# Places of their own for the sums and copies of the first channel product, and long rows for its weight sums in DRAM

## The chip, the cores and the metric

The kernel runs on one core of a Trainium2 chip. The metric is the device time of one execution in microseconds (us), as a median of several runs; less is better. The engines of a core are called here by the names that the profile uses: PE (TensorE, the matmuls; PEld are its weight loads), DVE (VectorE), ACT (ScalarE), POOL (GpSimd) and SP (SyncE, which here only issues DMAs). DMAs are issued by SP, by ACT and by POOL[...].

## What is computed

An attention block whose mask comes from hashes of the queries and keys, and after it an MLP mixer with a token part and a channel part. The change lies in the channel part, the last two lines:

```python
xt = x.transpose(0, 2, 1)                       # x: attention output, 4 x 768 rows of 512
h = np.maximum(xt @ w_tok1, 0.0) @ w_tok2       # token part
u = x + h.transpose(0, 2, 1)
h2 = np.maximum(u @ w_ch1, 0.0) @ w_ch2         # channel part: 512 -> 1536 -> 512
return (u + h2).astype(np.float32)
```

All data are float32. In the kernel u lies transposed in SBUF as the tile XT, 128 partitions by 4 blocks of channels by 3072 rows.

## The kernel before

Attention takes about the first 320 us, the token part follows until about 404 us, and the channel part, the function `channels`, runs from 404 us to the end. It works in three groups of 1024 rows (s = 0, 1, 2). Each group has two products: the first channel product (512 to 1536, then a ReLU, into the four tiles R) and the second (1536 to 512, in `outputs`).

**Fewer multiplications by sums.** Both products are split 2 x 2 in the manner of Strassen and Winograd: seven products of half-size blocks in place of eight, p1 to p7, with sums and differences of the weights on the one side, of the data on the other, and of the results. In groups 1 and 2 the first product is split a second time for four of its seven (p2, p6, p3, p4, the list `SMALLER`), and in all groups the second product is for six of its seven. The sums of weights for this second level are made once, in group 0, by DVE (`prepare`), and written to DRAM: `left_...` for the second product (`passed`), `hidden_left_...` for the first (`hidden_passed`). Later groups fetch them from there.

**Group 0** runs `hidden(0, t)` for six blocks t. A block has seven accumulations in PSUM; ACT copies three of the results (p1, p5, p7) and the sum u into SBUF (`copy`, L714 and L716), DVE adds them into R (L746, L755), POOL adds p5 and p7 (L750). In between, at two places for each t, DVE runs one of eleven jobs of `prepare`. A job of `parts` makes four sums (L986 to L989) in a place and hands it to a store. There are two such places: the tile `seen`, and, where `other` is true, a piece of `area(1)`. SP then issues the DMAs to DRAM: for the second weights L997 and L999, for the first L1006 (three DMAs for the sums, one for each t) and L1011 (four for the blocks that need no sum).

**Groups 1 and 2** run `hidden_pair(s, t)` for three t, each over two blocks at once. A pair computes p1 whole, then the four smaller products with a class `Smaller`, whose steps are `one`, `three`, `rest` and `finish`. `one` starts a bank of PSUM and lets ACT copy its first part into a place e (L827); `rest` lets PE add into the same bank, and then fetches the weight sums of the product that comes five later (`fetch_hidden_left`, L788), into one of five slots in WC1 and SW1. The copies of a pair are p1, p5 and u (L880), e2 and e6 (L827), and e3 and e4, which take the places of p1 and e2 again.

**Where they lie.** Two large SBUF tiles, area(0) and area(1), stand at the places that the second weights and their sums had (WC2 and SW2). Each holds, in its first 2688 columns, the weight sums of one of the six split products (`left_at`, filled by L1047 two products ahead, 1344 KB each), and behind them blocks of results: `output_at(0)`, `(1)` and `(2)` in area(0), `output_at(3)` in area(1), and behind that a scratch piece `extra`. In `outputs` these blocks are q7, q57 (later q4), q6 (later q3) and q5 (later q2). q57, q3, q2 and q4 are added to the output in DRAM by POOL's DMAs (L1151 in `store`), the last of them, q4, after the last product of a group, by L1186 and L1187:

```python
add(q4, q4, q7)()
store(q4, 1, 0)()
```

The next group's first pair then takes its places by

```python
p1, e2, u, e6, p5 = [output_at(i).rearrange("p i n -> p (i n)") for i in (0, 2, 3, 1)] + [flat_q1]
```

so that p1 is where q7 was, e2 where q3 was, u where q2 was, e6 where q4 was, and p5 where q1 was.

**What sets the order.** The program is written out in order by hand (`manual_schedule`): every engine takes its instructions in the order of the text, and an instruction waits until what it reads is written and what it overwrites has been read, by whatever engine or DMA. In pools, tiles of one tag share a number of places (`bufs`), and a new tile waits for the last use of the one that had its place. PSUM is cut into four pairs of banks that go round (`ring`). SP's queue holds nearly all fetches and stores in the order of the text. POOL's queue holds the stores of L1151 and the fetches of `look` (L1226): 384 KB of the queries or keys, which ACT squares and sums later (L1215, L1216), to find out whether the fast attention was safe. Were it not, a second, careful version of everything would run (the `If` at the end); with these inputs it does not.

Of the kernel before, what the change touches and what calls it, by code (L numbers as in the profile page):

```python
# [48 lines left out]
def kernel(  # L49
# [13 lines left out]
    nc = tc.nc  # L63
# [617 lines left out]
    def channels(pool, psum, SW1, second, TA, judge):  # L681
# [6 lines left out]
        q1 = pool.tile([P, KC, TT], F32, name="q1", tag="q1", bufs=1)  # L688
        last = B * S // (2 * TT) - 1

        def copies(name):
            return pool.tile([P, TT], F32, name=name, tag="c", bufs=6)


        ring = [0, 1, 2, 3]
# [15 lines left out]
                    skip_group_check=True,  # L711
                )

        def copy(ps, name, shape=None):  # L714
            c = copies(name)
            nc.scalar.copy(c if shape is None else shape(c), ps)  # L716
            return c if shape is None else shape(c)

        def split(a):
            return a.rearrange("p (n t) -> p n t", n=2)  # L720
# [8 lines left out]
        def hidden(s, t):  # L729


            sl = [slice(TT * (2 * s + i), TT * (2 * s + i) + TT) for i in range(2)]
            low, high = slice(P * t, P * t + P), slice(DCH // 2 + P * t, DCH // 2 + P * t + P)
            ks = range(KC)
            r = [a[:, :, t] for a in R]
            ps = [b[:, i] for b in blocks(2) for i in range(2)]
            accumulate(ps[0], lambda k: WC1[:, k, low], lambda k: XT[:, k, sl[0]], ks)
            accumulate(ps[1], lambda k: WC1[:, KC + k, low], lambda k: XT[:, KC + k, sl[0]], ks)
            accumulate(ps[2], lambda k: WC1[:, k, high], lambda k: T[0][:, k], ks)
            accumulate(ps[3], lambda k: SW1[:, 1, k, low], lambda k: T[2][:, k], ks)  # L740
            p1 = copy(ps[0], "p1")
            p5 = copy(ps[2], "p5")
            accumulate(ps[0], lambda k: SW1[:, 0, k, low], lambda k: T[1][:, k], ks, False)
            p7 = copy(ps[3], "p7")
            end_rows()
            nc.vector.tensor_tensor(r[0], split(ps[1]), split(p1), op=ALU.add)  # L746
            nc.vector.tensor_scalar(r[0], r[0], 0.0, None, op0=ALU.max)
            for job in jobs.pop(0) if jobs else []:
                job()
            nc.gpsimd.tensor_tensor(p7, p5, p7, op=ALU.add)  # L750
            accumulate(ps[2], lambda k: SW1[:, 2, k, low], lambda k: XT[:, KC + k, sl[1]], ks, False)
            accumulate(ps[3], lambda k: WC1[:, KC + k, high], lambda k: T[3][:, k], ks, False)
            u = copy(ps[0], "u")
            for k, a in [(3, p7), (1, ps[2]), (2, ps[3])]:
                nc.vector.tensor_tensor(r[k], split(a), split(u), op=ALU.add)  # L755
            nc.vector.tensor_scalar(r[1], r[1], 0.0, None, op0=ALU.max)

            def end():
                for k in (3, 2):
                    nc.scalar.activation(r[k], r[k], ACT.Relu)  # L760

            unfinished.append(end)
            nc.vector.tensor_tensor(r[1], r[1], r[0], op=ALU.subtract)
# [21 lines left out]
        def fetch_hidden_left(h):  # L785

            if h < 4 * GP * last:
                nc.sync.dma_start(out=hidden_left_at(h), in_=hidden_passed[SMALLER[h % 4]][:, h // 4 % GP, : 7 * P])  # L788

        def hidden_left_at(h):  # L790

# [14 lines left out]

        def kept(name):

            a = hidden_passed[name]
            return [a[:, :, P * i : P * i + P] for i in range(4, 8)]  # L810

        def rows_of(a):

            return a[:, 0].rearrange("p (t c) -> p t c", t=GP)

        class Smaller:

# [37 lines left out]
        def hidden_pair(s, t, between):  # L855


            sl = [slice(TT * (2 * s + i), TT * (2 * s + i) + TT) for i in range(2)]
            ks = range(KC)
            r = [a[:, :, t::GP].rearrange("p n i c -> p i n c") for a in R]  # L860
            x, z, e, y = ring
            ring[:] = [y, e, x, z]
            p1, e2, u, e6, p5 = [output_at(i).rearrange("p i n -> p (i n)") for i in (0, 2, 3, 1)] + [flat_q1]
            e3, e4 = p1, e2
            h = 4 * GP * (s - 1) + 4 * t
            p2, p6, p3, p4 = [Smaller(h + i, name, s) for i, name in enumerate(SMALLER)]

            def rows(a):
                return a.rearrange("p (i n c) -> p i n c", i=2, n=2)

            def banks(a):
                return a.rearrange("p i (n c) -> p i n c", n=2)

            def whole(pair, left, right, which=(0, 1)):
                for i in which:
                    at = P * (t + GP * i)
                    accumulate(pair[:, i], lambda k: left(k)[:, at : at + P], right, ks)

            def copy(to, pair):
                nc.scalar.copy(to.rearrange("p (i n) -> p i n", i=2), pair)  # L880

            def plus(to, a, b):
                nc.vector.tensor_tensor(to, a, b, op=ALU.add)

            def relu(i):
                nc.scalar.activation(r[i], r[i], ACT.Relu)

            X = bank_pair(x)
            whole(X, lambda k: WC1[:, k], lambda k: XT[:, k, sl[0]])
            Z, E = bank_pair(z), bank_pair(e)  # L890
            copy(p1, X)
            p2.one(E, e2)
            p2.three(Z, True)
            Y = bank_pair(y)
            whole(Y, lambda k: WC1[:, k, DCH // 2 :], lambda k: T[0][:, k], [0])
            n = TT * 3 // 2
            plus(p1[:, :n], Z.rearrange("p i n -> p (i n)")[:, :n], p1[:, :n])
            end_rows()
            p2.rest()
            whole(Y, lambda k: WC1[:, k, DCH // 2 :], lambda k: T[0][:, k], [1])  # L900
            p2.finish()
            copy(p5, Y)
            look()
            plus(r[0], rows(p1), rows(e2))
            for job in between:
                job()
            E = bank_pair(z)
            p6.one(E, e6)
            p6.three(X)
            copy(u, X)  # L910
            V = bank_pair(e)
            whole(V, lambda k: SW1[:, 1, k], lambda k: T[2][:, k])
            p6.rest()
            look()
            plus(rows(p5), banks(V), rows(p5))
            p6.finish()
            relu(0)
            plus(u, u, e6)
            E3 = bank_pair(x)
            p3.one(E3, e3)  # L920
            look()
            p3.three(Y)
            p4.three(V)
            p4.one(bank_pair(z), e4)
            plus(r[1], banks(Y), rows(u))
            plus(r[2], banks(V), rows(u))
            plus(r[3], rows(p5), rows(u))
            p3.rest()
            p4.rest()
            p3.finish()  # L930
            plus(r[1], r[1], rows(e3))
            p4.finish()
            plus(r[2], r[2], rows(e4))
            look()

            def end():
                relu(3)
                relu(1)
                relu(2)
                nc.vector.tensor_tensor(r[1], r[1], r[0], op=ALU.subtract)  # L940

            unfinished.append(end)
# [3 lines left out]
        SMALLER = ["p2", "p6", "p3", "p4"]  # L946
        GP = HC // 2
        hidden_passed = second["hidden_passed"]
        flat_q1 = q1.rearrange("p i n -> p (i n)")

# [7 lines left out]
        def prepare():  # L960
# [33 lines left out]
            def second_parts(name):  # L994
# [3 lines left out]
                    for i, a in enumerate(raw):  # L998
                        nc.sync.dma_start(out=to[:, 4 + i].rearrange("p (k c) -> p k c", k=QC), in_=a)  # L999

                return parts(left[name], store)

            def hidden_parts(name):
                def store(place, raw, rest):
                    for t in range(GP):
                        nc.sync.dma_start(  # L1006
                            out=hidden_passed[name][:, t, : 4 * P].rearrange("p (i c) -> p i c", i=4),
                            in_=place[:, :, P * t : P * t + P],
                        )
                    for there, here in zip(kept(name), [*raw, rest]):  # L1010
                        nc.sync.dma_start(out=there, in_=rows_of(here))  # L1011

                return parts(first_weight(name), store, SMALLER.index(name) % 2 == 0)

# [70 lines left out]
        def product(s, j, name, q, between, final=None):  # L1085
# [13 lines left out]

            part(0, 4, b00)  # L1100
            part(1, 5, b10)
            p1 = copy(ps[0], "p1", lambda c: c[:, half])
            nc.vector.tensor_tensor(b00, b11, b01, op=ALU.subtract)  # L1103
            part(2, 0, b01)
            part(3, 1, extra())
            nc.vector.tensor_tensor(b10, b10, b00, op=ALU.subtract)
            p57 = copy(pairs[1][:, :, half], "p57", lambda c: c.rearrange("p (i t) -> p i t", i=2))
            part(0, 2, b00, False)
            part(2, 3, b11, False)
            u = copy(ps[0], "u", lambda c: c[:, half])  # L1110
            if s < last:
                look()
            part(3, 6, b10, False)
# [133 lines left out]
        if not judge:  # L1247
            for name in SMALLER:
                (a00, a01), (a10, a11) = weight_quarters(first_weight(name))
                for there, here in zip(kept(name), [a00, a01, a11, a10]):  # L1250
                    nc.sync.dma_start(out=rows_of(here), in_=there)
        for t in range(HC):
            if t == 1:
                residual(0)
# [23 lines left out]
    def with_token_weights(stage):  # L1278
        with tc.tile_pool(name="tok", bufs=1, reuse_waits="tile") as tok:
# [7 lines left out]
    n = NHT // 4 * P  # L1287
    second = {
        "hidden_passed": {
            f"p{i}": dram.tile([P, NHT // 4, 8 * P], F32, name=f"hidden_left{i}") for i in (2, 3, 4, 6)  # L1290
        },
        "passed": {
            f"p{i}": dram.tile([P, (4 if i == 1 else 7) * n], F32, name=f"left{i}") for i in range(1, 8)
# [95 lines left out]
```

## Time and profile before

The median of three runs is 825.07 us (824.71 to 825.82). The profiled execution has a span of 823.8 us.

| engine | busy, us | share of the span | instructions |
|---|---|---|---|
| PE | 807.6 | 98% | 3901 |
| DVE | 665.2 | 81% | 869 |
| ACT | 423.4 | 51% | 675 |
| POOL | 42.6 | 5% | 69 |

| DMA issues of the part concerned | number | KB each |
|---|---|---|
| `second<-left` (L1047) | 18 | 1344 |
| `left<-seen` (L997) | 6 | 768 |
| `left<-second` (L999) | 18 | 192 |
| `hidden_left<-second`, `hidden_left<-seen` (L1006) | 6 + 6 | 256 |
| `hidden_left<-WC`, `hidden_left<-SW` (L1011) | 8 + 8 | 192 |
| `WC<-hidden_left`, `SW<-hidden_left` (L788) | 15 + 9 | 448 |
| `out<-second` from POOL (L1151) | 11 | 512 |

How to read it. In the names of the profile, `out<-in` is what an instruction writes and reads; buffer numbers are left out, so that `second` stands for area(0), area(1), WC2 and SW2 alike, `b` for the PSUM banks, `p` and `u` for the copies of `hidden` and `product`, and `q` for q1. A bracket at the end of a line of the timeline, such as [0.56 <-DVE R L1103], says how long the engine stood idle before this line, and what ended the wait. A part of a line that reads "x14" is a run of 14 instructions merged. A float32 matmul shows as two instructions. "To landing" is the time from the issue of a DMA to its completion.

### The profile page before, as it was taken

The page shows a single profiled execution, that of the slowest core. Times are in us where ns is not written, and L with a number is a line of the kernel's source. Part 1 is how long each engine was busy: PE and PEld are TensorE (multiplying, and loading weights), DVE is VectorE, ACT ScalarE, POOL GpSimd, SP SyncE. Part 2 cuts the span into 40 slices and gives each one's busy share as a digit, 9 for nine tenths or more (in the row PEclk, how much of TensorE's full clock was granted, in tenths as well). Part 3 has the DMA queues.
Part 4 walks back from the last instruction along what each step waited for, and adds up shares of the span by engine and source line. Part 5 has one row for each costly group of instructions (what it writes and reads, how often), then busy time and mean ns, then how long its engine had stood idle before and what let it go on. Part 6 is the DMA issues. An engine that isn't in the chain of part 4 may idle for free.

```text
span 823.8 us, 10610 instructions
## 1 busy us (share of the span) xinstructions
PE 807.6 (98%) x3901; PEld 473.6 (57%) x3901; DVE 665.2 (81%) x869; ACT 423.4 (51%) x675; POOL 42.6 (5%) x69
## 2 busy tenths in 40 slices
PE   9999999999999999999999999997999998999996
PEld 4444444444444444455544458865666885675885
DVE  4889898999988676798486869985769896777985
ACT  5777788888887774121022321335773333775111
POOL 1000000000000000000011110111100011100001
PEclk9999999999999999999999999999999999999999
DMA  4445454546524235561028895696644577630455
GB/s 159 140 142 169 136 156 138 162 156 207 146 89 118 80 79 189 173 212 39 0 76 293 245 329 191 197 311 179 239 143 141 222 202 179 224 121 1 148 182 112
DMA packets 79915, 132.31 MB, mean 161 GB/s; under 512 B 29608, under 2 KB 51568, under 8 KB 77552
## 3 DMA queue, kind: packets, MB, share of 16 engines
q1 hardware_dynamic: 73744, 112.60, 41.4%
q0 software_dynamic: 5552, 18.35, 9.1%
q8 instruction: 33, 0.54, 0.3%
q10 hardware_dynamic: 560, 0.61, 0.2%
q14 instruction: 26, 0.21, 0.1%
HBM read 97.21 MB, written 33.69 MB: 159 GB/s over the span
## 4 chain that ended last, share of the span: by engine, by line
PE 76%; issue 16%; DMA 2%; DVE 2%; POOL 2%; ACT 1%; POOLq 0%; ACTq 0%; DVEq 0%
PE b L709 28%; PE sc L345 19%; PE acc L392 16%; PE t L623 5%; PE t L642 5%; PE sums L416 2%; DMA out<-second 1%; PE hp L306 1%; DMA second<-left 1%; POOL seen L1226 1%; POOL out L1151 1%; DVE second L1145 1%; PE hw L324 0%; PE idle L454 0%; POOL looked L1226 0%
## 5 line engine op out<-in xcount | busy, mean ns | idle before, releaser
L352 ACT ACTIVATE e<-sc 128x768 f32<-128x768 f32 x192 | 153.1, 812 | 13.2 <-PE sc L345 12.3
L345 PE MATMUL sc<-qk 64*128 64x384 f32 x768 | 158.5, 492 | 0.3 <-ACT e L352 0.3
L709 PE MATMUL b<-R,second 128*128 128x256 f32 (+1 forms) x612 | 151.2, 404 | 1.1 <-DVE R L1103 0.6
L709 PEld LDWEIGHTS b<-R,second 128*128 128x128 f32 x612 | 116.1, 190 | 33.3 <-issue 18.6
L392 PE MATMUL acc<-e,vn 128*64 128x384 f32 x768 | 130.9, 490 | 0.0
L384 DVE TENSOR_TENSOR esd<-esd,e 128x768 f32<-128x768 f32 x128 | 122.3, 955 | 10.4 <-ACT e L352 0.5
L716 ACT COPY p<-b 128x512 f32<-128x512 f32 (+1 forms) x54 | 27.2, 516 | 158.3 <-PE b L709 158.3
L345 PEld LDWEIGHTS sc<-qk 64*128 64x128 f32 x768 | 66.5, 187 | 55.6 <-issue 45.2
L392 PEld LDWEIGHTS acc<-e,vn 128*64 128x64 f32 x768 | 52.3, 137 | 74.9 <-issue 74.3
L709 PE MATMUL b<-XT,WC 128*128 128x256 f32 (+1 forms) x264 | 84.2, 464 | 4.6 <-ACT second L827 4.6
L709 PEld LDWEIGHTS b<-XT,WC 128*128 128x128 f32 x264 | 51.2, 194 | 35.0 <-issue 24.6
L345 PE MATMUL sc<-bits 64*128 64x384 bf16 x384 | 62.9, 323 | 0.2 <-DVE bits L328 0.2
L623 PE MATMUL t<-x,W 128*128 128x512 f32 x96 | 41.8, 593 | 0.0
L642 PE MATMUL t<-W,r 128*128 128x384 f32 x128 | 41.8, 486 | 0.0
L398 ACT ACTIVATE num<-acc,vsum 128x384 f32<-128x384 f32 x32 | 18.6, 582 | 41.6 <-PE acc L392 41.2
L437 ACT COPY rec<-rec 32x384 f32<-32x384 f32 x64 | 32.6, 509 | 12.9 <-DVE rec L431 12.4
L709 PE MATMUL b<-XT,SW 128*128 128x256 f32 (+1 forms) x120 | 36.4, 440 | 2.1 <-ACT second L827 2.1
L380 DVE SCALAR_TENSOR_TENSOR esd<-e 128x768 f32<-128x768 f32 x32 | 30.5, 954 | 9.3 <-ACT e L352 9.3
L642 PEld LDWEIGHTS t<-W,r 128*128 128x128 f32 x128 | 24.3, 190 | 17.6 <-issue 1.4
L345 PEld LDWEIGHTS <-bits 64*128 64x128 bf16 x384 | 19.3, 94 | 25.4 <-DVE bits L328 0.8
L709 PE MATMUL b<-TA,WC 128*128 128x512 f32 x72 | 33.8, 592 | 0.0
L709 PE MATMUL b<-TA,SW 128*128 128x512 f32 x72 | 32.9, 592 | 0.0
(170 smaller groups left out, 1064.6 us busy)
## 6 DMA issues: line engine op xcount, KB each, us to landing
second<-left SPq DMA_DIRECT2D x18, 1344.0 KB
raw<-in_moe_w_ch SPq DMA_DIRECT2D x16, 768.0 KB
qk<-in_qk SPq DMA_DIRECT2D x15, 768.0 KB
seen<-in_qk POOLq DMA_DIRECT2D x21, 384.0 KB, 4.0
WC<-hidden_left SPq DMA_DIRECT2D x15, 448.0 KB
vn<-in_v SPq DMA_DIRECT2D x16, 384.0 KB
vt<-in_vT SPq DMA_DIRECT2D x16, 384.0 KB
bounced<-stage SPq DMA_DIRECT2D x32, 192.0 KB
```

The source lines that it names most:

```text
L345: nc.tensor.matmul(sc[:, i, :HALF], t[rows, 1, P * c : P * c + P], t[rows, 0, qs], start=start, stop=not start,)
L352: nc.scalar.activation(e, sc[:, :, :HALF], ACT.Exp, scale=SCALE)
L380: nc.vector.scalar_tensor_tensor(self.d, es[0], NR * EPS, es[1], op0=ALU.add, op1=ALU.add,)
L384: nc.vector.tensor_tensor(self.d, self.d, e, op=ALU.add)
L392: nc.tensor.matmul(acc[D * i : D * i + D], vn[:, i, c], e[:, i], start=(c == 0), stop=(c == NR - 1),)
L398: nc.scalar.activation(nums[self.n][:, self.half], acc, ACT.Identity, scale=-1.0, bias=vsum,)
L416: nc.tensor.matmul(ps[at : at + 32], ones[:, :32], self.halves[h].d[:, i], start=True, stop=True,)
L437: nc.scalar.copy(rec[other : other + 32, h], rec[at : at + 32, h])
L623: nc.tensor.matmul(ps, W1[:, r, P * j : P * j + P], x[:, r], start=(r == 0), stop=(r == NR - 1),)
L642: nc.tensor.matmul(ps[:, :HALF], r1[:, j, P * cb : P * cb + P], W2[:, j, HALF * half : HALF * half + HALF], start=(j == 0), stop=(j == NJ ...
L709: nc.tensor.matmul(ps, left(k), right(k), start=start and k == ks[0], stop=stop and k == ks[-1], skip_group_check=True,)
L716: nc.scalar.copy(c if shape is None else shape(c), ps)
```

## The change

It does four things.

1. The tag `c`, of which the copies are tiles, has 3 places of 1024 columns and no longer 6 of 512. A hidden block of group 0 takes two tiles and cuts each in half, for p1, p5 and p7, u. A product of `outputs` takes one and cuts it into p1 (a quarter), p57 (a half) and u (a quarter); before, it took three tiles.
2. In a hidden pair, p5, e6 and u are three such tiles. Only p1 and e2 (and e3 and e4 after them) stay in `output_at`.
3. The sums of p2 of the second weights are made in the piece of area(1) and not in `seen`, so that `seen` and the piece alternate from there on.
4. The DRAM tiles of the first product's weight sums are laid out as 8 rows of 384 columns in each partition, and no longer as 3 blocks of 8 x 128. A store of the sums is then one DMA with whole rows, a store of a block without sums has rows of 384 columns (1.5 KB), not of 128 (512 bytes); a fetch reads seven pieces of 128 columns for each partition, where it read 896 columns in one piece.

It is for the waits at the places that are stored from, and for the number of pieces that the stores to DRAM are cut into.

```diff
-        def copies(name):
-            return pool.tile([P, TT], F32, name=name, tag="c", bufs=6)
+        def copies():
+            return pool.tile([P, 2 * TT], F32, name="c", tag="c", bufs=3)
...
-        def copy(ps, name, shape=None):
-            c = copies(name)
-            nc.scalar.copy(c if shape is None else shape(c), ps)
-            return c if shape is None else shape(c)
+        def copy(ps, c):
+            nc.scalar.copy(c, ps)
+            return c
...
-            p1 = copy(ps[0], "p1")
-            p5 = copy(ps[2], "p5")
+            c = [a[:, TT * i : TT * i + TT] for a in (copies(), copies()) for i in range(2)]
+            p1 = copy(ps[0], c[0])
+            p5 = copy(ps[2], c[1])
...
-            p7 = copy(ps[3], "p7")
+            p7 = copy(ps[3], c[2])
...
-            u = copy(ps[0], "u")
+            u = copy(ps[0], c[3])
...
-                nc.sync.dma_start(out=hidden_left_at(h), in_=hidden_passed[SMALLER[h % 4]][:, h // 4 % GP, : 7 * P])
+                t = h // 4 % GP
+                nc.sync.dma_start(
+                    out=hidden_left_at(h).rearrange("p (i c) -> p i c", i=7),
+                    in_=hidden_passed[SMALLER[h % 4]][:, :7, P * t : P * t + P],
+                )
...
-            a = hidden_passed[name]
-            return [a[:, :, P * i : P * i + P] for i in range(4, 8)]
+            return [hidden_passed[name][:, i] for i in range(4, 8)]
...
-            p1, e2, u, e6, p5 = [output_at(i).rearrange("p i n -> p (i n)") for i in (0, 2, 3, 1)] + [flat_q1]
+
+            p1, e2 = [output_at(i).rearrange("p i n -> p (i n)") for i in (0, 2)]
+            p5, e6, u = copies(), copies(), copies()
...
-                return parts(left[name], store)
+                return parts(left[name], store, name == "p2")
...
-                    for t in range(GP):
-                        nc.sync.dma_start(
-                            out=hidden_passed[name][:, t, : 4 * P].rearrange("p (i c) -> p i c", i=4),
-                            in_=place[:, :, P * t : P * t + P],
-                        )
+                    nc.sync.dma_start(out=hidden_passed[name][:, :4], in_=place)
                     for there, here in zip(kept(name), [*raw, rest]):
-                        nc.sync.dma_start(out=there, in_=rows_of(here))
+                        nc.sync.dma_start(out=there, in_=here[:, 0])
...
-            p1 = copy(ps[0], "p1", lambda c: c[:, half])
+            c = copies()
+            p1 = copy(ps[0], c[:, half])
...
-            p57 = copy(pairs[1][:, :, half], "p57", lambda c: c.rearrange("p (i t) -> p i t", i=2))
+            p57 = copy(pairs[1][:, :, half], c[:, TT // 2 : TT * 3 // 2].rearrange("p (i t) -> p i t", i=2))
...
-            u = copy(ps[0], "u", lambda c: c[:, half])
+            u = copy(ps[0], c[:, TT * 3 // 2 :])
...
-            f"p{i}": dram.tile([P, NHT // 4, 8 * P], F32, name=f"hidden_left{i}") for i in (2, 3, 4, 6)
+            f"p{i}": dram.tile([P, 8, NHT // 4 * P], F32, name=f"hidden_left{i}") for i in (2, 3, 4, 6)
```

More of the change, by code (lines that the diff above doesn't have):

```diff
@@ L807, in kept @@
         def kept(name):
-            a = hidden_passed[name]
-            return [a[:, :, P * i : P * i + P] for i in range(4, 8)]
-        def rows_of(a):
-            return a[:, 0].rearrange("p (t c) -> p t c", t=GP)
+            return [hidden_passed[name][:, i] for i in range(4, 8)]
         class Smaller:
@@ L948, in channels @@
         hidden_passed = second["hidden_passed"]
-        flat_q1 = q1.rearrange("p i n -> p (i n)")
         ORDER = ["p1", "p5", "p7", "p6", "p3", "p2", "p4"]
@@ L1250, in channels @@
                 for there, here in zip(kept(name), [a00, a01, a11, a10]):
-                    nc.sync.dma_start(out=rows_of(here), in_=there)
+                    nc.sync.dma_start(out=here[:, 0], in_=there)
         for t in range(HC):
```

## The prediction

> **What bounds the kernel now.** I read the engines' busy time first, then the stretches in which TensorE is not full, then who ended each gap.
>
> The profile page, part 1 and one line of part 5 (idle before it and releaser at the right):
>
> ```profile
> PE 807.6 (98%) x3901; PEld 473.6 (57%) x3901; DVE 665.2 (81%) x869; ACT 423.4 (51%) x675; POOL 42.6 (5%) x69
> ...
> L709 PE MATMUL b<-XT,WC 128*128 128x256 f32 (+1 forms) x264 | 84.2, 464 | 4.6 <-ACT second L827 4.6
> ```
>
> TensorE (PE) is the bound, so the change is worth what PE stands idle, plus what a slow clock costs after a gap. The busy time by stretch (start:end, length, then PE, weight load, VectorE, ScalarE, GpSimd, granted clock, DMA share, GB/s):
>
> ```profile
> 470.00:480.00 10.00, 10.00 (x24) 4.37 (x23) 3.95 (x8) 2.71 (x5) 2.37 (x2) 1.00 1.04 303
> 480.00:500.00 20.00, 18.90 (x72) 13.20 (x71) 18.77 (x27) 3.69 (x7) 1.10 (x2) 1.00 1.06 340
> ...
> 540.00:560.00 20.00, 17.66 (x59) 10.69 (x57) 14.76 (x25) 6.59 (x11) 3.60 (x4) 1.00 0.91 262
> 560.00:580.00 20.00, 17.75 (x62) 12.96 (x63) 12.51 (x14) 13.91 (x23) 1.66 (x3) 0.91 0.70 234
> ...
> 680.00:700.00 20.00, 17.89 (x56) 10.77 (x56) 13.00 (x24) 7.30 (x13) 3.57 (x4) 0.96 0.75 184
> ```
>
> From 380 us to 800 us PE is otherwise full in every row. It lacks 1.10 us at 480 to 500, 2.34 + 2.25 = 4.59 us around 560, and 2.11 us before 700; the clock falls just after the last two. The timeline names the releasers (start, length, engine, what):
>
> ```profile
> 492.38 4.12 PE L709 MATMUL b<-R,second 128*128 128x256 f32 x18 [0.56 <-DVE R L1103]
> 497.05 4.12 PE L709 MATMUL b<-R,second 128*128 128x256 f32 x18 [0.55 <-DMA second<-left]
> ...
> 555.61 1.21 POOL L1151 DMA_DIRECT2D out<-second  x1 [7.34 <-DVE XT L775]
> 561.82 0.37 ACT L827 COPY second<-b 128x256 f32<-128x256 f32 x1 [6.47 <-DMA out<-second]
> 562.25 4.83 PE L709 MATMUL b<-XT,WC 128*128 128x256 f32 x14 [4.59 <-ACT second L827]
> ...
> 691.58 1.21 POOL L1151 DMA_DIRECT2D out<-second  x1 [8.82 <-DVE second L853]
> 697.59 0.37 ACT L827 COPY second<-b 128x256 f32<-128x256 f32 x1 [4.00 <-DMA out<-second]
> 698.02 4.98 PE L709 MATMUL b<-XT,SW 128*128 128x256 f32 x14 [2.12 <-ACT second L827]
> ```
>
> Read upwards, the big gaps are one chain, once at each of the two group boundaries. GpSimd issues the adding store of block q4 (L1151 for L1187) at 555.61; it lands at about 561.75, since the chain of waits has a piece of 6.13 us for it (5.93 us at the second). ScalarE's copy for e6 (L827, from p6.one) goes to `output_at(1)`, the place that q4 is stored from, so it waits. PE's p6.rest adds into the bank that this copy reads, so PE waits too.
>
> [...] a gap of 2.12 us also costs clock here, so I count both. [...] at 470 to 480, mostly 512-byte stores, 303 GB/s at a share of 1.04. No line here shows a 512-byte read from DRAM.
>
> **Part 1: e6, u and p5 in tiles of their own (L863).** e6 leaves q4's place, u leaves q2's (`output_at(3)`), p5 leaves q1. Same copies, same sizes: no work added. When would e6's copy start? ScalarE's work before it, the second half of a look, starts at 555.17 and takes 0.19, so it is free at 555.36; the copy takes 0.37 and ends about 555.8. PE ends its eight 512-wide matmuls (554.07, 3.60 long) at 557.66. So e6 is ready 1.9 us early and the gap closes: 4.6 us, and 2.1 us at the second boundary. The clock: 14 matmuls of 256 columns took 4.83 and 4.98 us; 12 in full clock take 2.75 (at 613.41), so 14 take 3.2. That is 1.6 + 1.8 = 3.4 us more.
>
> What waits next? I walked the pair on. The u copy ends at 556.8 and a look at 558.8, when p6.rest is through (559.0); the three copies of p6, p3 and p4 then end before PE asks, as in the pairs for t = 1, 2, where PE has no gap. e2 stays in `output_at(2)`, from which q3 is stored: issued 535.15, median landing 7.5 us, 542.7; e2 is copied at 547.03, 4.3 us to spare. The three new tiles were last read by the product before (L1137, done 544.78); p5's copy is at 552.54. No wait.
>
> **Part 2: copies as halves and quarters of 3 tiles of 1024 instead of 6 of 512.** Same bytes and instructions. A product now uses one tile of three, not three of six. A hidden block uses two of three, so a tile returns after 1.5 blocks, as before. ScalarE's u waited for L746 (16.4 us in 5 waits), the reader of p1: apparently it took p1's slot. It now shares a tile with p7 instead. PE was full all through 400 to 480, so: nothing.
>
> **Part 3: sums of p2 (second weights) to area(1).** VectorE's sums wait for the previous store of the one place "seen": five waits, 11.3 us in all. Two alternating places shorten this. The new wait is for the old tile of area(1), SW2: its last store is issued by 444.92 and p2's sums ran at 450.92, so 6 us to spare (a similar store released VectorE 3.3 us after issue). Behind these sums on VectorE stand the adds of the hidden block (L746, L755), and PE waits for those only a block (12 us) later. Worth nothing by itself.
>
> **Part 4: long rows for the hidden sums' stores.** Per name: before, 3 + 4 issues with 12 x 128 + 4 x 384 = 3072 rows of 512 B; after, 1 + 4 issues with 128 rows of 6 KB and 512 of 1.5 KB. SyncE (SP) time falls from 4.46 us (1.81 + 2.65 at 484.46) to about 5 x 0.33 = 1.7, by the 0.33 us of a 128-row issue. This touches the first gap. VectorE sat 6.43 us at 480.96 for a hidden store, and L1103 ended 0.56 us late. SP issued the last hidden store until 488.96, and only then (489.07) the fetch of p7's weights, which took 7.85 us and came 0.55 late; p1's matmuls, which free its place, end about 486.6. With VectorE 6 us and the fetch 2.4 us earlier both waits close: 1.1 us. No clock loss there.
>
> **Part 5: the price, reads in 512-byte pieces (L788).** 24 fetches of 448 KB (459 KB decimal) go from 128 rows of 3.5 KB to 896 of 512 B. Lower bound: 459 KB at 414 GB/s (545 to 550, full DMA) = 1.1 us. Upper bound: one row costs the same however short, 7 times that, 7.8 us; the stores speak against it (303 GB/s). I take the stores' rate: 1.5 us, and keep 3.0 as a doubtful end. PE uses up one fetch in 5.6 us (two pairs, 8 fetches, from 571.23 to 616.00 = 44.8 us); four others lie ahead in the ring; DMA share at 580 to 620 is 0.60 and 0.48. Even 3.0 us a fetch fits. The first five are issued from 532.65 behind a fetch of 768 KB (786 KB decimal); at 229 GB/s (532 to 536) the first lands at about 538.5, and is used at about 546. SP needs about 1 us for each, from the 0.57 us of a 512-row store: hidden, its next issue is at 542.64. What hides the cost: PE's own work.
>
> **Sum.** 1.1 + 4.6 + 2.1 + 3.4 = 11.2 us. I keep 0.3 for short waits of the kind of PEld on L850 (0.7 us in three). 825.07 - 10.9 = **814.2 us**.
>
> **Rivals.**
> (a) All gaps close: 814.2. Chance 0.76.
> (b) Another wait takes over in part: the pairs begin earlier, but a look's data may not. The look fetched at 556.37, behind q4's store, would be wanted at 565.5, not 571.70; at its median landing of 6.4 us it comes at 562.8, at the longest of 7.9 still in time. ScalarE runs its queue in order, so a late one holds the copies behind it. If each boundary keeps 1.5 us, 814.2 + 3 = 817.2, or 818.9 with one clock loss. For it: DMA is full (1.03) at 545 to 550. Chance 0.14.
> (c) Nothing gained: the copies still wait for the store through the way that the three tiles are handed out, and part 4 alone counts: 824. Against: the tiles' readers are done 8 us before. Chance 0.03.
> (d) Short reads are the new bound, slower: at three times the stores' cost, 4.5 us a fetch, nine fetches in 540 to 580 add some 9 x 3.1 = 28 us of DMA time where only 40 x 0.195 = 8 us are free; if three quarters of that 20 us reach PE, 814.2 + 15 = 829. Chance 0.07.
>
> **Numbers.** Faster 0.76 + 0.14 + 0.01 of (c) = 0.91; same 0.02; slower 0.07. The range runs from 813.0 (nothing kept back, a run's spread) to 819.0, the end of (b).
>
> **What would show it.** Right: no wait of ScalarE's L827 on `out<-second`, PE full at 540 to 580 and 680 to 700 with clock 1.00, the p7 fetch issued near 486.6, no VectorE wait on hidden_left, DMA share in the pairs up by no more than a tenth. Wrong: PE waiting for `WC<-hidden_left` or `SW<-hidden_left`, or ScalarE waiting for `seen` and `looked` at their squares (L1215), or e2's copy waiting for q3's store.

## The result, and the profile after

The changed kernel takes **813.68 us** (813.58 to 814.83), the kernel before 824.97 us beside it: a ratio of 0.9865, with a 95% interval of 0.9847 to 0.9882. That is 11.3 us less; 814.2 us was forecast. The experiments below ran on other chips, on which the kernel before took some 826.5 us with a wider spread. So they are read by their ratio to it and, where single microseconds matter, by the gaps in their profiles.

The profile page of the changed kernel, part 1 and the line of part 5 that showed the wait:

```profile
PE 803.6 (99%) x3901; PEld 471.6 (58%) x3901; DVE 664.1 (82%) x869; ACT 423.1 (52%) x675; POOL 42.5 (5%) x69
...
L709 PE MATMUL b<-XT,WC 128*128 128x256 f32 (+1 forms) x264 | 82.5, 456 | 0.0
```

The span fell from 823.8 to 811.9, by 11.9 us. PE's idle time, the span less its busy time, went from 16.2 to 8.3: 7.9 us, against 7.8 us of gaps forecast to close. Its busy time for the same 3901 matmuls fell by 4.0. Of this, 3.5 us lie in the two lines of part 5 that hold the 14 matmuls after the big gaps (XT,WC from 84.2 to 82.5, XT,SW from 36.4 to 34.6): the clock that the gaps had cost, with a granted clock of 0.91 at 560 to 580 and 0.96 at 680 to 700 before and of 1.00 in both now. The other 0.5 us is within the spread of kernels that have none of the gaps, whose PE busy times run from 802.6 to 804.0.

The stretches, in the columns of the prediction (PE's busy time is the second number):

```profile
470.00:480.00 10.00, 10.00 (x25) 4.49 (x24) 6.66 (x12) 3.97 (x7) 1.96 (x2) 1.00 0.99 388
480.00:500.00 20.00, 20.00 (x78) 14.60 (x77) 15.81 (x21) 2.71 (x5) 1.10 (x2) 1.00 0.68 238
...
540.00:560.00 20.00, 20.00 (x71) 13.10 (x70) 15.29 (x27) 10.60 (x19) 4.17 (x5) 1.00 0.92 242
560.00:580.00 20.00, 20.00 (x70) 13.10 (x69) 14.14 (x16) 14.21 (x24) 1.94 (x4) 1.00 0.99 314
...
680.00:700.00 20.00, 20.00 (x74) 13.87 (x73) 16.26 (x24) 13.36 (x23) 3.46 (x5) 1.00 0.89 213
```

PE is full at a clock of 1.00 in each. At 470 to 480 the DMA engines move 388 GB/s at about the share that gave 303 before. How much of that is the long rows isn't shown: the long rows alone, tried below, gave 317 there.

At the first boundary the timeline reads (lines of ACT, PE and POOL, in order of time):

```profile
545.63 0.38 ACT L826 COPY second<-b 128x256 f32<-128x256 f32 x1
...
553.87 0.35 ACT L826 COPY c<-b 128x256 f32<-128x256 f32 x1
...
556.11 3.19 PE L709 MATMUL b<-XT,WC 128*128 128x256 f32 x14
...
556.64 1.21 POOL L1148 DMA_DIRECT2D out<-second  x1 [11.53 <-issue]
...
564.98 0.84 ACT L1212 ACTIVATE looked<-looked 128x768 f32<-128x768 f32 x1 [0.96 <-DMA looked<-in_qk]
```

e6 (L826, now into c) is copied at 553.87, before q4's store is even issued (556.64), and PE goes on at 556.11 without a bracket. Its 14 matmuls take 3.19 us where they took 4.83. The first line is e2, still in q3's old place, the last a look that came 0.96 us late; both come up again.

The chain of waits from 440 to 805 us is now PE alone:

```profile
439.62 329.04 PE b L709 x1226
768.66 0.11 PE b L1235
768.77 36.28 PE b L709 x168
```

### The profile page after: what moved, and what is told of

The parts are those of the page before. It is cut to its first block, busy times and chain, and to the rows that moved or that the text cites. A ratio compares the mean times of both kernels' runs of the same rounds, so it can differ in the third digit from the quotient of the medians.

```text
span 811.9 us, 10567 instructions
## 1 busy us (share of the span) xinstructions
PE 803.6 (99%) x3901; PEld 471.6 (58%) x3901; DVE 664.1 (82%) x869; ACT 423.1 (52%) x675; POOL 42.5 (5%) x69
## 3 DMA queue, kind: packets, MB, share of 16 engines
q1 hardware_dynamic: 82320, 112.60, 42.4%
## 4 chain that ended last, share of the span: by engine, by line
PE 99%; DVE 0%; ACT 0%; issue 0%; ACTq 0%
PE b L709 49%; PE sc L345 20%; PE acc L392 16%; PE t L623 5%; PE t L642 5%; PE sums L416 2%; PE hp L306 1%; PE hw L324 1%; PE idle L454 0%; ACT vt L297 0%; ACT e L352 0%; ACT g L311 0%; DVE second L1128 0%; DVE g L310 0%; DVE bits L326 0%
## 5 line engine op out<-in xcount | busy, mean ns | idle before, releaser
L715 ACT COPY c<-b 128x512 f32<-128x512 f32 (+1 forms) x78 | 37.4, 488 | 187.7 <-PE b L709 174.2
L709 PE MATMUL b<-XT,WC 128*128 128x256 f32 (+1 forms) x264 | 82.5, 456 | 0.0
L437 ACT COPY rec<-rec 32x384 f32<-32x384 f32 x64 | 32.6, 509 | 12.9 <-DVE rec L431 12.4
L709 PE MATMUL b<-XT,SW 128*128 128x256 f32 (+1 forms) x120 | 34.6, 422 | 0.0
```

Of the source, the lines that this page charges most:

```text
L437: nc.scalar.copy(rec[other : other + 32, h], rec[at : at + 32, h])
L709: nc.tensor.matmul(ps, left(k), right(k), start=start and k == ks[0], stop=stop and k == ks[-1], skip_group_check=True,)
L715: nc.scalar.copy(c, ps)
```

## The experiments

The theory is that of the prediction: e6's place held PE at both boundaries, and the stores of the hidden weight sums held the fetch of p7's weights. The first rival is that less work for the DMA engines let q4's store land in time; the second, that u or p5 was the holder; the third, that the short reads cost something.

**The places alone, and the rows alone.** The first kernel is the changed one without its parts 3 and 4, the second the kernel before with these two alone.

```diff
# places alone, against the changed kernel
-                    out=hidden_left_at(h).rearrange("p (i c) -> p i c", i=7),
-                    in_=hidden_passed[SMALLER[h % 4]][:, :7, P * t : P * t + P],
+                nc.sync.dma_start(out=hidden_left_at(h), in_=hidden_passed[SMALLER[h % 4]][:, h // 4 % GP, : 7 * P])
...
-                return parts(left[name], store, name == "p2")
+                return parts(left[name], store)
```

> The new places and the tiles of 1024 alone (parts 1 and 2); rows in DRAM and the place of p2's sums as before. Theory: the two large gaps and the clock loss after them go, the first gap (1.1 us at 480 to 500) stays: 825.0 - 10.1 = about 814.9, with the p7 fetch still issued near 489. Rival (the DMA relief of the long rows is what lets the store of q4 land in time): about 824, with ScalarE still waiting for the store.

> Long rows and p2's place alone (parts 3 and 4); the sums and copies of the pairs stay in the stored blocks. Theory: only the first gap closes, and the store of q4 lands a little later because the fetches now read 512-byte pieces: between 824 and 827, and perhaps slower than before. Rival (DMA relief closes the gaps): near 814.

Measured: the places alone, ratio 0.9872 (0.9836 to 0.9908); the rows alone, 0.9984 (0.9973 to 0.9996). PE's timeline, first with the places alone, then with the rows alone:

```profile
497.44 2.83 PE L709 MATMUL b<-R,second 128*128 128x256 f32 x12 [1.26 <-DMA second<-left]
```

```profile
562.91 5.50 PE L709 MATMUL b<-XT,WC 128*128 128x256 f32 x14 [6.79 <-ACT second L826]
...
698.83 3.29 PE L709 MATMUL b<-XT,SW 128*128 128x256 f32 x14 [1.59 <-ACT second L826]
```

With the places alone the first gap stays, and it is the only one. With the rows alone it goes, and the two others stay. They shift, from 4.59 and 2.12 to 6.79 and 1.59 us. At the first boundary PE asks 1.5 us earlier (556.12 for 557.66), and q4's store is issued 1.1 us later (556.75 for 555.61), because q2's store before it took 12.4 us to land, 8.2 in the kernel before. So relief of the DMA engines did not bring q4's store in time; the first rival falls. The first gap is too small to be seen in the times: the places alone lie within the interval of a repeat of the whole change on the same chip, below (0.9855, 0.9813 to 0.9898).

**Which place.** The changed kernel with e6 back, with u back, and with u and p5 back:

```diff
-            p1, e2 = [output_at(i).rearrange("p i n -> p (i n)") for i in (0, 2)]
-            p5, e6, u = copies(), copies(), copies()
# e6 back
+            p1, e2, e6 = [output_at(i).rearrange("p i n -> p (i n)") for i in (0, 2, 1)]
+            p5, u = copies(), copies()
# u back
+            p1, e2, u = [output_at(i).rearrange("p i n -> p (i n)") for i in (0, 2, 3)]
+            p5, e6 = copies(), copies()
# u and p5 back
+            p1, e2, u = [output_at(i).rearrange("p i n -> p (i n)") for i in (0, 2, 3)]
+            p5 = q1.rearrange("p i n -> p (i n)")
+            e6 = copies()
```

> The changed kernel with e6 alone back in q4's place. Theory: e6 is the one copy that holds. In the changed kernel q4's store lands at 563.5 (556.6 + 6.9) and at 689.7 (683.7 + 6.0), the matmuls before it end at 556.1 and 688.0: gaps of about 7.7 and 2.2 us, and 1.7 us of clock after each, so about 827, slower than before the change. Rival (u's or p5's place was the holder): 813.7, no gap.

> The changed kernel with u alone back in q2's place. The store of q2 lands at 556.3 (543.9 + 12.4), u is copied at 554.1 in the changed kernel: ScalarE is held 2.2 us at the first boundary; at the second q2's store lands at 683.4, before u at 686.0: no wait. Theory: up to 1.5 us of PE gap, 813.7 to 816. Rival (u's place is worth as much as e6's): 820 or more.

> The changed kernel with p5 back in q1 and u back in q2's place: of the pairs' copies only e6 has a place of its own. Theory: the whole gain of the two large gaps is e6's, so this is the changed kernel's time (813.7 to 815 on the first chip), with ScalarE held about 1.4 us for u at the first boundary and PE full. Rival (p5 or both places count): 816 or more.

Measured: e6 back, ratio 0.9976 (0.996 to 0.9992); u back, 0.9849 (0.9815 to 0.9883); u and p5 back, 0.9847 (0.9823 to 0.9871). PE with e6 back:

```profile
562.63 6.00 PE L709 MATMUL b<-XT,WC 128*128 128x256 f32 x14 [6.66 <-ACT second L826]
...
699.29 3.29 PE L709 MATMUL b<-XT,SW 128*128 128x256 f32 x14 [1.84 <-ACT second L826]
```

ACT with u and p5 back, the copy of u:

```profile
555.31 1.01 ACT L882 COPY second<-b 128x1024 f32<-128x1024 f32 x1 [1.52 <-DMA out<-second]
```

e6's place alone makes or breaks the gain of the two large gaps. u does wait for q2's store when it lies there, 1.5 us, and PE does not notice; its span is 811.9 us, that of the changed kernel. The size was missed for e6 back: 827 was expected, which is a span of some 825.2 (the time less 1.8 us); the profile has 823.1. The store landed at 562.1 and not 563.5, and the second gap, 1.84 us, cost no clock (1.00 at 680 to 720). The sum of the spans does close: 811.9 + 6.66 + 1.84 + 2.8 (14 matmuls in 6.00 instead of 3.19) = 823.2.

**What closes the first gap.** The kernel before with the long rows alone (part 4 of the change, as its diff shows it), with p2's place alone (part 3), and the changed kernel without the long rows (parts 1 to 3):

```diff
# p2's place alone, against the kernel before
-                return parts(left[name], store)
+                return parts(left[name], store, name == "p2")
```

> Only the rows in DRAM changed (part 4), p2's sums and all copies where they were. Theory: the first gap is the long stores' doing, so it closes (no wait of VectorE above 2 us for hidden stores, the p7 fetch issued near 486.7, PE full at 480 to 500); the later gaps as with both (6.8 and 1.6 us): 823 in the profile. Rival (the place of p2's sums closes it): about 1.1 us of gap at 480 to 500 stays.

> Only p2's sums moved to the piece of area(1) (part 3). Theory: VectorE waits less for the stores of the second weights (11.3 us before, about 8.7 with it), but the short rows still hold the last hidden job and the issue of the p7 fetch: the gap at 480 to 500 stays at 0.5 to 1.3 us, 824 in the profile. Rival: the gap closes.

> The changed kernel with the old layout in DRAM (parts 1 to 3, short rows stored, 3.5 KB read in one piece). Moving p2's sums alone closed the first gap, and so did the long rows alone. Theory: either is enough, so the time of the changed kernel, PE full at 480 to 500. Rival (with PE earlier the short stores hold the p7 fetch again): a gap of 0.5 to 1.3 us at 497.

Measured: long rows 0.9987 (0.9967 to 1.0008), inconclusive as a time; p2's place 0.9968 (0.9952 to 0.9985); parts 1 to 3, 0.9848 (0.9827 to 0.9869), as good as the whole change. The row 480 to 500 of each:

```profile
480.00:500.00 20.00, 20.00 (x72) 13.49 (x71) 18.81 (x27) 3.61 (x6) 1.10 (x2) 1.00 0.87 330
```

```profile
480.00:500.00 20.00, 20.00 (x76) 14.14 (x75) 18.74 (x26) 3.88 (x7) 1.10 (x2) 1.00 0.96 310
```

```profile
480.00:500.00 20.00, 19.96 (x80) 14.80 (x79) 17.36 (x23) 2.72 (x5) 1.10 (x2) 1.00 0.86 289
```

The third expectation held, the second failed: p2's place alone closes the gap too. The first held in the main, but VectorE still waits 3.6 us for the hidden stores there (6.4 before), not under 2. With p2's place alone it waits 2.3.

The same work stands up to 4 us apart in these traces, so times are counted from the first matmul of the second product. With p2's place, and then with the long rows alone, this matmul and SP's issue of p7's fetch read:

```profile
477.56 14.35 PE L709 MATMUL b<-R,second 128*128 128x512 f32 x42
...
488.06 0.48 SPq L1047 DMA_DIRECT2D second<-left  x1
```

```profile
479.18 14.35 PE L709 MATMUL b<-R,second 128*128 128x512 f32 x42
...
489.68 0.32 SPq L1042 DMA_DIRECT2D second<-left  x1
```

The fetch is issued 10.5 us after that matmul in both, as in every run without the gap (10.5 in the changed kernel, with the rows alone and with parts 1 to 3). It is 12.9 us in the kernel before (489.07 - 476.18) and 13.0 with the places alone. So each part brings the fetch forward by the whole 2.4 us, to where the matmuls of p1 leave its place free, and no part can bring it further. With p2's place SP is done with the hidden stores only 0.2 us before (487.86), with the long rows 2.5 us (487.20). The parts are not additive: each closes the same 1.1 us, and the second one adds nothing.

**The price of short reads.** First, each fetch cut into 14 pieces in each partition:

```diff
-                    out=hidden_left_at(h).rearrange("p (i c) -> p i c", i=7),
-                    in_=hidden_passed[SMALLER[h % 4]][:, :7, P * t : P * t + P],
+                    out=hidden_left_at(h).rearrange("p (i c) -> p i c", i=14),
+                    in_=hidden_passed[SMALLER[h % 4]][:, :7, P * t : P * t + P].rearrange(
+                        "p i (j c) -> p i j c", j=2
+                    ),
```

> The changed kernel with every fetch of the first product's weight sums cut into 256-byte pieces, 14 for each partition in place of 7. In the trace the 256-byte packets of other transfers took 18.6 ns and the 512-byte ones 29, so a fetch should cost 112 x 18.6 = 2.1 us of all engines in place of 56 x 29 = 1.6. Theory: still hidden, 813.7 to 815; the stores of q2 and q4 and the looks land a little later. Rival (short reads are close to being the bound): 818 or more, with PE waiting for the weights or ScalarE for the looks.

The trace has the same 21,504 packets of 512 bytes as the changed kernel, and the DMA share at 540 to 580 is 0.96 in both: neighbouring halves were joined again, so this is a repeat (0.9855, 0.9813 to 0.9898) and says nothing of the price. The changed kernel itself was run again with the third group above:

> The changed kernel as it is, on the same chip as the two others, to compare them by: 813.7 if this chip is like the first; the two others within 1 us of it.

It gave 0.985 (0.9828 to 0.9871), and u and p5 back, and parts 1 to 3, lie within 0.4 us of its median. The short reads were then tried with pieces that do not lie side by side. These reads bring as many bytes, but from other columns, so the kernel goes without the right weight sums, and only its time counts:

```diff
-                    out=hidden_left_at(h).rearrange("p (i c) -> p i c", i=7),
-                    in_=hidden_passed[SMALLER[h % 4]][:, :7, P * t : P * t + P],
+                    out=hidden_left_at(h).rearrange("p (i c) -> p i c", i=28),
+                    in_=hidden_passed[SMALLER[h % 4]][:, :7].rearrange("p i (j t c) -> p (i j) t c", j=4, t=GP)[:, :, t],
```

> The changed kernel with each fetch of the first product's weight sums read as 28 pieces of 128 bytes for each partition, three pieces apart in DRAM, so that they can't be joined (the pieces of 256 bytes in the earlier run lay side by side and were joined). The bytes are as many, but they belong to other columns, so the weights of groups 1 and 2 are not the right ones; only the time is of interest. 448 KB are then 3584 pieces, 224 for each of 16 engines. The trace shows 18.6 ns for a 256-byte packet and 29 for one of 512; a line through the two gives 13.4 ns for 128 bytes, so 3.0 us a fetch in place of 1.6, the doubtful end of the prediction. Theory: PE uses up one fetch in 5.6 us, so it stays hidden but for late looks and stores: 813.7 to 817, no wait of PE for the weights. Rival (at two to three times the cost short reads are the bound, as the prediction's slower case has it): 820 or more, with PE waiting for the fetches.

Measured: 0.9849 (0.9811 to 0.9887). The stretches 540 to 600:

```profile
540.00:560.00 20.00, 20.00 (x71) 13.10 (x70) 15.22 (x27) 10.74 (x18) 4.17 (x5) 1.00 1.15 189
560.00:580.00 20.00, 20.00 (x71) 13.10 (x70) 13.85 (x16) 14.12 (x24) 2.16 (x4) 1.00 1.30 237
580.00:600.00 20.00, 20.00 (x71) 13.10 (x70) 14.24 (x17) 14.75 (x25) 1.63 (x3) 1.00 1.19 261
```

These pieces stayed apart: the queue of the fetches has 146,832 packets where the changed kernel has 82,320, three times 21,504 more. Its share of the engines' time is 48.5% of 810.6 us for 42.4% of 811.9; from that, if the other packets took as long in both, a 128-byte packet took about 16.4 ns, an estimate. A fetch then took 224 x 16.4 = 3.7 us, 2.3 times the 1.6 us of the changed kernel (56 x 29.2 ns). The DMA share goes to 1.30 at 560 to 580, so the times of packets overlap, and at 540 to 580 fewer bytes move than in the changed kernel (189 and 237 GB/s for 242 and 314); they follow at 580 to 600 (261 for 152). PE stays full all the same, and no wait of PE or ACT on a DMA is left between 500 and 750. At 2.3 times the cost the rival falls; where short reads would become the bound was not measured.

**Why q4's store comes so late.** Its data are ready 7 to 12 us before POOL issues it (before, at the first boundary, VectorE's L1145 ends at 546.05, and the issue is at 555.61). In both kernels and at both boundaries it went out 0.3 us after q2's store had landed (before: 547.07 + 8.2 = 555.3, issued 555.61). Tested on the kernel before, with one place fewer for the copies to make space:

```diff
-            return pool.tile([P, TT], F32, name=name, tag="c", bufs=6)
+            return pool.tile([P, TT], F32, name=name, tag="c", bufs=5)
...
-        "TRN2", target_bir_lowering=False, num_devices=1, dynamic_dma_scratch_size=1024
+        "TRN2", target_bir_lowering=False, num_devices=1, dynamic_dma_scratch_size=2048
```

> The kernel before with twice the room for the descriptors of GpSimd's DMAs (2048 bytes for 1024) and, to make space, five places for the copies in place of six. In both kernels q4's store was issued 0.3 us after q2's had landed, though its data were ready some 9 us earlier. If the room for descriptors is what it waits for: it is issued near 548 and lands by about 557, the copy of e6 hardly waits, both gaps shrink to under 1 us: 815 to 817. Rival (a wait of another kind, on data or on the output): no difference, 825.

Measured: 0.9891 (0.9852 to 0.9929), span 819.1. POOL's stores of q2 and q4, and then PE:

```profile
544.51 1.21 POOL L1151 DMA_DIRECT2D out<-second  x1
547.75 1.21 POOL L1151 DMA_DIRECT2D out<-second  x1 [2.03 <-DVE XT L775]
```

```profile
561.54 4.97 PE L709 MATMUL b<-XT,WC 128*128 128x256 f32 x14 [2.54 <-ACT second L827]
```

The store goes out 3.2 us after q2's and does not wait for its landing. So, as far as this run shows, it waited for room in the scratch space that `dynamic_dma_scratch_size` sets; the releasers that the profile had named there, additions of VectorE, were not. The sixth place for the copies was not taken away alone, so no run excludes that it has a share in this. But with two stores in flight at the first boundary each takes 13.3 to 13.8 us to land, and q4's lands only at about 561. The second gap is gone, the first shrinks to 2.54 us and not to under 1: half of the mechanism. As a time the ratio makes it 816.0 on the first chip, within the 815 to 817 that were expected, though the profiled run was the slowest of its four.

## Why the prediction was right, point by point

- **e6 (4.6 + 2.1 us): right.** Its copy is done at 554.2, 1.9 us before PE asks, as worked out. The runs with e6 back and with e6 alone show that the two large gaps hang on this place.
- **The clock (3.4 us): right.** The two lines with the 14 matmuls fell by 1.7 and 1.8 us.
- **The first gap (1.1 us): right size, wrong step.** "Worth nothing by itself", of p2's place, failed: it closes the gap alone, and the long rows are then worth nothing. The sum did not suffer, since both are in the change. Also wrong was SP's time for the last hidden store, "about 1.7": its five issues took 0.32 + 3.54 = 3.9 us, the last four 0.77 to 0.91 us each and not 0.33; why stays open. It did no harm because they began 8 us earlier (476.51 in place of 484.46). The fetch went out at 486.86 (486.6 forecast).
- **Reads of 512 bytes (1.5 us a fetch): right**, 1.6 by the packets. Three times the cost, the slower rival's case, was not reached; but by that rival's working the 3.7 us of the 128-byte pieces, for 1.4 in the kernel before (8 x 170 ns), would have cost 9 x 2.3 - 8 = 13 us of DMA time too many, and three quarters of it in PE. Measured: none. The step of the rival that fell is to count DMA time beyond the free share as PE time; the transfers that came later had slack.
- **Rows of 512 bytes: slower than long ones.** The prediction took 303 GB/s at a share of 1.04, at 470 to 480, for the rate of 512-byte stores; of the 3.0 MB that moved there, 1.3 MB were in such packets. Its own full stretch, 545 to 550, has 414 GB/s at 1.03, and the packets show 17.5 GB/s for each engine at 512 bytes, 21 at 3,584. The price of a fetch came out right because it was reckoned with the measured 303.
- **The DMA share in the pairs: a sign that failed.** It was to rise by no more than a tenth. At 560 to 580 it went from 0.70 to 0.99, at 680 to 700 from 0.75 to 0.89; at 580 to 620 it changed by a tenth at most (0.55 and 0.58 for 0.60 and 0.48). PE was full in each, so the sign was no sign of harm.
- **e2's margin (4.3 us): too large, and misread.** A median of 7.5 us was taken for q3's store, but the trace of the kernel before has 11.6 us for this very store: it landed at about 546.8, 0.3 us before e2's copy at 547.03. In the changed kernel it took 10.0 us, landed at 543.6, and e2 was copied at 545.63: 2.0 us. That this wait did not take over was in part luck.
- **Late looks (rival b): the wait came, not its price.** ACT waited 0.96 us once for a look; PE did not.
- **u and p1's slot: fallen.** With u in another tile ACT still waits for L746, 12.0 us in five waits (16.4 before). Nor was a place taken: u waits 1.44 us already in the first block, in both kernels, when no place has been used before. What holds u there stays open; it costs PE nothing.

The 0.3 us kept back was not needed: the sum without it is 11.2 us, and the times give 11.3. The 11.9 us between the profiles compares one execution of each kernel, and is no better a measure.

## What to carry to other kernels

Before a buffer is reused, ask who still reads it, a store to DRAM included: one 128 x 256 copy into a block whose store was late held PE twice, and a place of its own for that copy was the whole gain of some 10 us at the two boundaries. Walk from the gap to the wait that ends last, and give room there; when several edits relieve the same small wait, the first one takes it all. Fetches that ran several products ahead of their use were made some 2.3 times dearer here at no cost, while one fetch that came 0.55 us late held PE.

## What was not expected of the hardware

- **The clock after short gaps.** In the runs here, gaps of PE of 1.59 (the rows alone), 1.62 (p2's place), 1.84 (e6 back) and 1.86 us (long rows) were followed by 14 matmuls in 3.29 us, with a granted clock of 1.00 at 680 to 720; without a gap they take 3.19. After gaps of 2.12 and 4.59 (the kernel before), 2.54 (the larger scratch space) and 4.35 us (p2's place) the same 14 took 4.83 to 4.98, after 5.57 (long rows), 6.66 (e6 back) and 6.79 us (the rows alone) 5.50 to 6.20. In the kernel before the granted clock stands at 0.50 for 3.41 us with each of its two gaps, from 561.98 and from 698.51. At 560 to 580 its mean was 0.91 with the gaps of 2.54, 4.35 and 4.59 us, and 0.83 with those of 5.57 to 6.79: 0.17 of 20 us is 6.8 us at half the clock, an estimate. Matmuls all through 3.41 us at half the clock lose 1.7 us: the gap of 2.12 us cost 4.98 - 3.19 = 1.8 us more, nearly its own length again.
- **Not the length alone.** The gap of 5.57 us was followed by 14 matmuls in 6.20 us, that of 6.66 by 6.00 and that of 6.79 by 5.50: the longer gap cost less. And in the kernel before the first slow stretch begins at 561.98, 0.27 us before PE goes on, the second at 698.51, 0.49 us after it has gone on. What sets these moments is not shown here, nor what decides between 1.86 us, which cost no clock, and 2.12, which did.
- **Short pieces.** In the changed kernel 512-byte packets of reads took 29.2 ns and those of stores 29.1, about 17.5 GB/s for each engine; packets of 3,584 bytes in the kernel before took 170 ns, 21 GB/s. Seven times as many pieces thus cost only some 20% more DMA time. These are means beside other traffic; the medians, 27 and 140 ns, make it 35%.
- **GpSimd's stores one at a time.** With `dynamic_dma_scratch_size` at 1024 the second 512 KB store of a boundary was issued 0.3 us after the first had landed; with 2048, at the first boundary, 3.2 us after the first was issued, and both ran. There each then took 13.3 to 13.8 us in place of 8.2 and 6.1, at the second 9.0 to 9.4 in place of 9.7 and 5.9.
